# A halved K load, an earlier maximum and a finer last weight load in a decode-attention kernel that streams 1.08 GB

## Chip, cores, metric

One core of a Trainium2 chip. The metric is the time of one execution in device microseconds (us).

Names: PE is TensorE's matmul row, DVE is VectorE, ACT ScalarE, SP SyncE, which issues nearly every load. A timeline line reads: start in us, length in us, engine, line of the kernel, operation, output<-inputs, shapes, how many, and in brackets the idle time before it and what ended it. PEq, DVEq and SPq are the engines' sequencers, the parts that wait for semaphores.

## The reference, cut to what matters

```python
x = A_x                                     # 1 x 448
xn = _layernorm(x)
q = (xn @ wq) in 16 heads of 256            # one query per head
scores = q . k_cache * 256**-0.5            # k_cache: 16 x 65536 x 256, bf16
o = softmax(scores) . v_cache               # v_cache: the same size
g = silu(silu(xn @ w1) @ w2)
return x + (o @ wo) * g
```

K and V are 537 MB each and are read once. Each head is cut into four blocks of 16384 keys, 64 blocks in all, 8 MiB of K and 8 MiB of V per block.

## The kernel before

Three buffers `R[0..2]` of 8 MiB hold everything. A K block is multiplied in place by VectorE and summed by VectorE and ScalarE; then its V block is loaded over it, TensorE multiplies V by the weights, and the next K block but two is loaded over that. So a K load waits for a V product (`vf`), and a V load for VectorE (`kf`).

```python
def load_k(i, s):
    take(sp, vf[s])                          # SyncE waits: V product of this buffer done
    sp.dma_start(out=R[s][:, :], in_=block(Kd, i)).then_inc(kl[s], 16)
    sp.sem_inc(kh[s], 16)                    # kl: first half there, kh: second half there

def load_v(i, s):
    take(sp, kf[s])                          # VectorE is done with this K block
    sp.dma_start(out=R[s][:, :], in_=block(Vd, i)).then_inc(vl[s], 16)

def pe_v(s):
    take(pe, pv)
    take(pe, vl[s], 16)
    pe_keys(psO, s, s, 0, KB, True, True, od)    # 64 matmuls, two keys a partition each
    pe_mark().then_inc(vf[s], 1)

def pe_max(i):
    pe_rows()              # waits for VectorE's maxima of block i, puts them in one row
    pe_query(i + 1)        # the next block's query, which VectorE needs to start it
    pe_bcast()             # waits for the maximum over the row, sends it to ScalarE

# SyncE
load_k(2, 2); load_v(0, 0); load_v(1, 1)
with nc.Fori(NR, LAST - 2, NR, ...) as i:    # NR = 3, LAST = 63
    for s in range(NR):
        load_k(i + s, s)
        load_v(i + s - 1, (s - 1) % NR)
# ... (last K in halves, last V blocks in pieces) ...
pieces = cuts(0, 5, 10, 14, 16)              # wo's heads, one load and semaphore for each piece

# TensorE
pe_max(0)
with loop(pe, 1, LAST - 2, NR) as i: ...     # pe_turn, pe_max(i), pe_v(s) for three blocks
pe_block(NBLK - 3, 0)
pe_turn()
pe_v(1)                                      # V product of block 61
pe_max(NBLK - 2)                             # maximum of block 62, query of block 63
# ... at the very end, after the last V product:
project(10, 12); pe_turn(...); project(12, 14); project(14, 15); project(15, 16)
```

A block has KB = 128 keys in each partition, and HK is half of that. `pe_turn` transposes the last output row, so head 15 can be projected only after it.

## Time and profile before

| what | before |
|---|---|
| time, median of the first 3 runs | 2521.9 us (2521.62 to 2524.93) |
| span of the traced run | 2521.1 us |
| bytes read | 1084.3 MB, 430 GB/s over the span |
| VectorE busy | 89% |
| an 8 MiB block behind another one | 19.36 us |
| last wo landing, last projection ended | 2514.94, 2516.96 us |

The page has 40 equal slices of 63 us. A slice's GB/s says how full the queue was; that of 433 is what the stream reaches with no hole.

A landing below is an issue's time plus its time to landing.

### The profile page before, as it was taken

To read this page: it belongs to the slowest core of one execution; us is meant where nothing else is said; L and a number is where in the kernel's file an instruction comes from. 1 tells how busy PE (TensorE), PEld (TensorE's weight loads), DVE (VectorE), ACT (ScalarE), POOL (GpSimd) and SP (SyncE) were. 2 spreads that over 40 slices of the span, in tenths; PEclk is the share of its full clock that TensorE was granted. 3 is DMA by queue.
4 is the path that set the end of the run, shared out by engine and by line. 5 is a ranking of instruction groups with operands and counts; after the bars stand their busy time and mean duration, and the time that the engine had idled before them with its cause. 6 is when DMAs were issued, how large, how long until landed. Compare 5 with 4: busy or idle time off the path is not lost. (4 is left out here: it accounts for less than half of the span.)

```text
span 2521.1 us, 29267 instructions
## 1 busy us (share of the span) xinstructions
PE 1151.9 (46%) x4738; PEld 438.2 (17%) x4738; DVE 2233.4 (89%) x10277; ACT 1445.9 (57%) x6996; POOL 1.9 (0%) x14
## 2 busy tenths in 40 slices
PE   3243544534535435345354353453543534534457
PEld 1111211111112112111121121121211211111122
DVE  6979889889898898898988988989989889889897
ACT  4656556556565565565655655655556556556564
POOL 0000000000000000000000000000000000000000
PEclk7666767767667677677676676766766767767678
DMA  9999999999999999999999999999999999999998
GB/s 424 402 433 433 433 433 433 434 432 433 435 434 436 435 436 434 434 433 434 435 433 433 433 433 433 433 433 433 433 436 435 436 436 434 434 433 435 433 423 353
DMA packets 22872, 1084.50 MB, mean 430 GB/s; under 512 B 2371, under 2 KB 4549, under 8 KB 4933
## 3 DMA queue, kind: packets, MB, share of 16 engines
q1 hardware_dynamic: 22850, 1084.30, 99.6%
q8 instruction: 5, 0.08, 0.0%
q14 instruction: 15, 0.11, 0.0%
q10 hardware_dynamic: 2, 0.00, 0.0%
HBM read 1084.29 MB, written 0.00 MB: 430 GB/s over the span
## 5 line engine op out<-in xcount | busy, mean ns | idle before, releaser
L276 ACT ACTIVATE R<-R 128x256 bf16<-128x256 bf16 x3328 | 1330.7, 401 | 754.4 <-ACTq L159 754.3
L254 DVE CUSTOM_DVE_ANT_0 R<-R,qcur 128x256 bf16<-128x256 bf16 x4864 | 1700.2, 417 | 0.0
L323 PE MATMUL bank<-R,PV 128*2 128x512 bf16 x4096 | 1032.1, 419 | 20.9 <-PEq L159 7.6
L243 DVE TENSOR_TENSOR R<-R,qcur 128x3328 bf16<-128x3328 bf16 x256 | 482.6, 1885 | 190.0 <-DVEq L159 189.9
L276 ACT ACTIVATION_READ_ACCUMULATOR R<-R 128x1 f32 x3328 | 619.9, 186 | 0.0
L335 PE MATMUL bank<-ident,rmax 128*1 128x128 bf16 x65 | 17.1, 263 | 1078.9 <-PEq L159 1078.9
L323 PEld LDWEIGHTS bank<-R,PV 128*2 128x2 bf16 x4096 | 367.3, 90 | 657.7 <-issue 218.4
L254 DVE DVE_READ_ACCUMULATOR2_ANT S<- 128x1 f32 x4864 | 384.1, 79 | 0.0
L335 PEld LDWEIGHTS bank<-ident,rmax 128*1 128x1 bf16 x65 | 5.2, 79 | 1083.4 <-issue 1083.3
L352 PE MATMUL bank<-eye,O 2*128 2x2 f32 x264 | 40.0, 252 | 231.3 <-PEq L159 231.3
L289 ACT ACTIVATE hist<-bank 128x1 f32 (+1 forms) x65 | 11.1, 171 | 204.4 <-ACTq L159 204.4
L352 PEld LDWEIGHTS bank<-eye,O 2*128 2x128 f32 x264 | 36.2, 207 | 248.6 <-issue 248.6
L219 DVE TENSOR_REDUCE gmax<-bank 1x1 bf16<-1x128 f32 x65 | 18.3, 281 | 38.1 <-DVEq L159 38.1
L236 DVE CAST qcur<-bank 128x256 bf16<-128x256 f32 x64 | 27.2, 425 | 24.6 <-DVEq L159 24.5
L310 ACT COPY hist<-bank 128x2 f32 (+1 forms) x66 | 10.5, 160 | 59.8 <-ACTq L159 59.8
L302 ACT COPY O<-bank 2x512 f32<-2x512 f32 x67 | 37.5, 559 | 12.4 <-ACTq L159 12.4
L291 ACT ACTIVATE PV<-S,hist 128x128 bf16<-128x128 f32 (+1 forms) x65 | 26.0, 399 | 13.4 <-ACTq L159 13.2
L366 PE MATMUL bank<-q,ident 8*128 (+1 forms) x63 | 24.3, 386 | 7.6 <-issue 1.7
L229 DVE COPY S<-S 128x128 f32<-128x128 f32 (+1 forms) x65 | 14.7, 226 | 9.5
L230 DVE TENSOR_REDUCE rmax<-S 128x1 bf16<-128x128 f32 (+1 forms) x65 | 18.2, 279 | 0.0
L341 PE MATMUL bank<-gmax,ones_row 1*128 1x1 bf16 x65 | 10.3, 158 | 4.6 <-PEq L159 0.9
L291 ACT ACTIVATION_READ_ACCUMULATOR PV<-S,hist (+1 forms) x65 | 12.1, 186 | 0.0
(68 smaller groups left out, 90.6 us busy)
## 6 DMA issues: line engine op xcount, KB each, us to landing
R<-in_A_k_cache_dram SPq DMA_DIRECT2D x4, 4096.0 KB, 24.2
R<-in_A_v_cache_dram SPq DMA_DIRECT2D x6, 2048.0 KB, 21.5
R<-in_A_wq_dram SPq DMA_DIRECT2D x1, 3072.0 KB, 12.7
R<-in_A_v_cache_dram SPq DMA_DIRECT2D x3, 1024.0 KB, 15.2
R<-in_A_wo_dram SPq DMA_DIRECT2D x2, 1120.0 KB, 18.4
R<-in_B_w_dram SPq DMA_DIRECT2D x1, 1568.0 KB, 27.1
R<-in_B_w_dram SPq DMA_DIRECT2D x1, 1344.0 KB, 5.8
R<-in_A_v_cache_dram SPq DMA_DIRECT2D x2, 512.0 KB, 16.4
```

Source lines behind the costliest of these rows:

```text
L219: dve.reduce_max(out=gmax[0:1, :], in_=ps_m[0:1, :], axis=AX.X).then_inc(gm, 1)
L230: dve.reduce_max(out=rmax[:, :], in_=S[:, c0:c1], axis=AX.X).then_inc(rm, 1)
L236: dve.tensor_copy(out=qcur[:, :], in_=ps_q).then_inc(sd, 1)
L243: m = dve.tensor_tensor(out=pair, in0=pair, in1=qcur[:, None, :].to_broadcast([P, NA, Dh]), op=ALU.mult,)
L254: ins = dve.tensor_tensor_reduce(out=Kv[:, c, :], in0=Kv[:, c, :], in1=qcur[:, :], scale=1.0, scalar=0.0, op0=ALU.mult, op1=ALU.add, accum ...
L276: ins = act.activation(out=prod, in_=prod, func=ACT.Identity, accum_out=S[:, c : c + 1],)
L291: act.activation(out=PV[s][:, c0:c1], in_=S2[:, c0:c1], func=ACT.Exp, bias=col(0, 1), scale=scale, accum_out=col(1, 2),).then_inc(pv, 1)
L302: act.copy(out=O[:, :], in_=po).then_inc(oc, 1)
L323: ins = pe.matmul(po, lhsT=PV[t][:, c : c + 2], rhs=R[s][:, c * Dh : (c + 2) * Dh], start=(start and c == k0), stop=(stop and c == k1 - 2),)
L335: pe.matmul(ps_m[0:1, :], lhsT=rmax[:, 0:1], rhs=ident[:, :], start=True, stop=True).then_inc(tm, 1)
L352: ins = pe.matmul(ps_t2[:, 2 * a : 2 * a + 2], lhsT=Ov[:, j, a, :], rhs=eye2[:, j, :], start=(j == 0), stop=(j == 1), is_transpose=True,)
L366: pe.matmul(ps_q, lhsT=ident[0:HP, at(j)].to_broadcast([HP, P]), rhs=q8[:, o : o + Dh] if isinstance(o, int) else q8[:, bass.ds(o, Dh)], s ...
```

## The change

Its intent: keep the queue filled at the one place where it ran empty, and shorten what follows the last landing. Diff, cut:

```diff
+    vh = [sem(f"vh{t}") for t in range(NR)]          # half a V product done
-    pieces = cuts(0, 5, 10, 14, 16)
+    pieces = cuts(0, 5, 10, 12, 14, 16)

-    def load_k(i, s):
+    def load_k(i, s, h=None):
+        if h is not None:
+            take(sp, h)
         take(sp, vf[s])

-    def pe_v(s):
+    def pe_v(s, k=KB, between=None):
...
-        pe_keys(psO, s, s, 0, KB, True, True, od)
+        pe_keys(psO, s, s, 0, HK, True, False, vh[s])
+        pe_keys(psO, s, s, HK, k, False, k == KB, od if k == KB else None)
+        if between:
+            between()
+            pe_keys(psO, s, s, k, KB, False, True, od)

-        with nc.Fori(NR, LAST - 2, NR, ...) as i:
+        take(sp, vh[0])
+        load_keys(R[0], block(Kd, NR), 0, HK, kl[0])     # fourth K block, first half
+        take(sp, vf[0])
+        load_keys(R[0], block(Kd, NR), HK, KB, kh[0])
+        load_v(2, 2)
+        for s in range(1, NR):                           # rest of the first pass, unrolled
+            load_k(NR + s, s, vh[s])
+            load_v(NR + s - 1, s - 1)
+        with nc.Fori(2 * NR, LAST - 2, NR, ...) as i:

-        with loop(pe, 1, LAST - 2, NR) as i: ...
-        pe_block(NBLK - 3, 0)
+        loop(pe, 1, NBLK - 3, NR, pe_block, more=1)      # leaves after one block of its last pass
         pe_turn()
-        pe_v(1)
-        pe_max(NBLK - 2)
+        pe_v(1, 96, lambda: pe_max(NBLK - 2))

-        project(h0, h0 + 2)
+        project(h0, h0 + 1)
         t = pe_turn(tok=True)
...
+        project(*pieces[3])
+        pe.wait_ge(wl[4], 16)
+        project(pieces[4][0], H1)
```

## The prediction

> **What bounds the kernel now.** I read the page's slices first, then the DMA queue's issues in order of time, stretches of 5 us in the first 200 us, the chain of waits, and the last 90 us engine by engine. The slices:
>
> ```profile
> DMA  9999999999999999999999999999999999999998
> GB/s 424 402 433 433 433 433 433 434 432 433 435 434 436 435 436 434 434 433 434 435 433 433 433 433 433 433 433 433 433 436 435 436 436 434 434 433 435 433 423 353
> HBM read 1084.29 MB, written 0.00 MB: 430 GB/s over the span
> ```
>
> The queue carries 433 GB/s nearly everywhere; VectorE, the busiest engine, has 89% and waits for K blocks. So the kernel is bound by moving 1084 MB, and only the slices that fall short can give anything: slice 2 (402), a little of slice 1, and the last two. 1084.3 MB at 433 GB/s is 2504 us; 2521.1 leaves 17 us for start, holes and end. A change that moves no bytes can take only a part of these 17 us, 0.7%.
>
> The hole in slice 2, by the queue's issues and in stretches (columns: span, busy time of PE, PEld, DVE, ACT, POOL, PEclk, DMA share, GB/s):
>
> ```profile
> 60.32 35.82 SPq L202 DMA_DIRECT2D R<-in_A_v_cache_dram  x2
> 117.81 0.35 SPq L197 DMA_DIRECT2D R<-in_A_k_cache_dram  x1
> ...
> 110.00:115.00 5.00, 5.00 (x25) 1.96 (x24) 5.00 (x27) 3.15 (x16) 0.00 (x0) 1.00 1.00 433
> 115.00:120.00 5.00, 3.12 (x17) 1.45 (x15) 5.00 (x24) 1.43 (x6) 0.00 (x0) 1.00 0.73 262
> 120.00:125.00 5.00, 0.00 (x0) 0.00 (x0) 5.00 (x20) 4.95 (x26) 0.00 (x0) 0.52 0.98 419
> ```
>
> The V block issued at 95.8 was the last thing in the queue. The fourth K block is issued only at 117.81, when the V product of block 0 (next fence, 100.64 to 117.5) has freed its buffer. By then the queue runs dry.
>
> ```profile
> 100.64 16.86 PE L323 MATMUL bank<-R,PV 128*2 128x512 bf16 x64 [3.59 <-PEq L159]
> 117.34 0.17 PE L376 MATMUL bank<-ident 128*1 128x1 bf16 x1
> ```
>
> The end, first TensorE and then VectorE:
>
> ```profile
> 2445.57 16.88 PE L323 MATMUL bank<-R,PV 128*2 128x512 bf16 x64 [2.96 <-PEq L159]
> 2462.29 0.17 PE L376 MATMUL bank<-ident 128*1 128x1 bf16 x1
> 2462.32 0.22 PE L335 MATMUL bank<-ident,rmax 128*1 128x128 bf16 x1
> ...
> 2506.51 7.07 PE L323 MATMUL bank<-R,PV 128*2 128x512 bf16 x32
> 2513.87 0.92 PE L699 MATMUL bank<-R,OT 128*1 128x448 bf16 x4 [0.29 <-DMA R<-in_A_wo_dram]
> 2514.72 0.64 PE L352 MATMUL bank<-eye,O 2*128 2x2 f32 x4
> 2515.28 1.68 PE L699 MATMUL bank<-R,OT 128*1 128x448 bf16 x8
> ```
>
> ```profile
> 2459.59 0.28 DVE L230 TENSOR_REDUCE rmax<-S 128x1 bf16<-128x128 f32 x1
> 2462.68 0.28 DVE L219 TENSOR_REDUCE gmax<-bank 1x1 bf16<-1x128 f32 x1 [2.81 <-DVEq L159]
> 2463.83 0.43 DVE L236 CAST qcur<-bank 128x256 bf16<-128x256 f32 x1 [0.87 <-DVEq L159]
> 2464.29 1.89 DVE L243 TENSOR_TENSOR R<-R,qcur 128x3328 bf16<-128x3328 bf16 x1
> ```
>
> ```profile
> 2495.95 17.87 DMA R<-in_A_wo_dram
> ```
>
> VectorE has block 62's maximum at 2459.87, but TensorE is in block 61's V product until 2462.3, so the last block starts at 2464.29. From 2506.51 TensorE works without a pause, and the wo piece with four heads lands at 2513.82, within 0.3 us of TensorE's being ready. The chain of waits names the transfer, but two chains end together there: the queue, and VectorE's last block followed by TensorE's last products. Shortening one alone would gain almost nothing.
>
> **What the Trainium skill says.** [...]the late K block took 23.0 us from issue to landing, where block follows block at 19.36 us (landings of 8 MiB blocks in the stretch after it), so 3.7 us are not its bytes, some of them the rest of the V block ahead. "TensorE: Matmul & The Clock Gate", section "What's actually happening", says that the array's clock falls to half after about 3.4 us of idleness; in this trace 1.98 us idle before 2481.74 was followed by a granted clock of 0.55, while 1.81 us before 2501.88 kept 1.00. "Runtime: NRT & Kernel Launch", section "Instruction fetch mechanics", says that a taken branch to a page that is not held stalls the engine. VectorE's 0.87 us idle before 2463.83, as it leaves its loop, may be one; this trace can't prove it.
>
> **The change part by part.**
>
> 1. Halved fourth K block. The half semaphore comes after 32 of the 64 matmuls. The first run at half clock: stretches of 5 us from 100 hold 11 and 21 of these matmuls, so the 32nd ends near 110. The first 4 MiB are then issued at about 110, some 8 us earlier, while the V block runs to 120.1. The second half is issued at 117.8 as before, behind 9.7 us of backlog. The hole closes. Its size in two ways: V1 lands at 120.11 (95.81 + 24.3), K3 at 140.84 (117.81 + 23.0), that is 20.7 us after it and not 19.36: 1.4 us. By bandwidth, 115 to 120 lacks 171 of 433 GB/s: 2.0 us. I take 1.6 us. VectorE also starts that block on its first half, at about 133 rather than 140.97; its 7.6 us of waiting move to the next K block, as the queue sets the pace from then on. All later landings move 1.6 us earlier.
>
> 2. Maximum ahead. Block 62's maximum, now ready at 2459.87 - 1.6 = 2458.3, is taken after 48 of block 61's 64 matmuls. Those began at 2445.57 - 1.6 and the last 16 take 3.5 us, so the 48th ends near 2457.3: TensorE waits 1 us, too short by the trace for a clock drop. VectorE's last block starts 1.97 us (2464.29 - 2462.32) after that row product, at about 2460.4 and not at 2464.3: 3.9 us earlier, 1.6 from the stream and 2.3 from this part. The 16 matmuls left end 2.1 us later relative to the stream; they free the buffer of the last V block, whose loads are issued behind three blocks' halves and pieces and land 27 us later, so that costs nothing. VectorE's end, hence TensorE's end chain, is ready 3.3 to 3.9 us earlier, and TensorE then waits for the last V pieces instead of for VectorE.
>
> 3. wo in three parts. The last V piece landed at 2494.83 + 16.8 = 2511.6; it now lands near 2510.0. Four matmuls of 0.22 follow, then ScalarE's copy (0.57, from 0.13 after), so the transposes start about 1.8 us after the landing, at 2511.9, and not at 2514.72. Meanwhile head 10 needs only its own two-head piece, about 1.1 us behind the V piece. After the transposes (0.6) come ten projections rather than eight, 0.21 each: end near 2514.6. The last two-head piece, landed at 2496.56 + 18.4 = 2514.95 before, lands near 2513.35; four products after it end at 2514.3. The later of the two, 2514.6, stands against 2516.97 before: 2.4 us.
>
> 4. One more block in TensorE's loop replaces 70 unrolled matmul-class instructions by a compare and branch in each of its passes, 20 of them. Between V products TensorE idles (17.41 us before a row product), so this costs nothing. SyncE gets one more wait per K block, already satisfied: nothing.
>
> Sum: 1.6 us of stream plus about 0.8 us of end, 2.4 us, not 1.6 + 2.3 + 1: parts 2 and 3 only let the end follow the queue. 2521.9 - 2.4 = 2519.5 us.
>
> **Rivals.**
> (a) Only the stream gains: the end stays TensorE's, because VectorE's early start is eaten by ScalarE, which must still copy block 61's output (now later) before it sums the last block. For it: ScalarE works in order. Against: it idles 3 us between groups of sums. Then 1.6 us: 2520.3.
> (b) The end gains in full and the hole too (2.0 us plus 1.3): 2518.5. Against: the last wo piece lands when the queue delivers it.
> (c) TensorE's new branches stall on instruction fetch behind a full queue at the loop's exit, now just before block 61's product. It has about 5 us (2438.95 to 2445.4) before V arrives; a longer stall would delay VectorE's last block and take back part 2: 2521 to 2522.
> (d) Holes reopen in the steady stream because K's release waits on two semaphores. Against: a block in the stretch from 193 us takes 25 us from issue to landing, a backlog of some 2 us. A microsecond per pass would be 20 us, 2540; unlikely.
>
> **Range and chances.** The three runs before span 3.3 us, more than the expected gain, so the range is set by noise and by rivals (a) to (c): 2517.3 to 2522.0. 2% is 50 us, three times all that lies outside the stream, so faster by over 2% is as good as excluded (0.003); slower needs rival (d) several times over (0.007); within 2%: 0.99.
>
> **What would show it.** Step 1: 4 MiB issued near 110 us, slice 2 near 420 GB/s or more, VectorE's fourth block starting near 133. Step 2: the last row product before the last 16 matmuls of block 61; VectorE's last block starting near 2460.4. Step 3: transposes near 2511.9, and last projections within 0.5 us of the last landing plus 0.9. Step 4: no idle time of TensorE over 3 us at its branch. I am wrong if slice 2 stays near 402, if the last landing doesn't move by 1 to 2 us, or if the end keeps its 2.0 us between last landing and last projection.

## The result, and the profile after

| | before | changed |
|---|---|---|
| first median | 2521.98 us (4 runs) | 2521.62 us (4 runs) |
| ratio | | 0.9998 (0.998 to 1.0015) |
| all runs, median | 2522.01 us (31 runs) | 2521.47 us (14 runs) |
| span of the traced run | 2521.1 us | 2519.0 us |

A ratio is the mean time of one kernel's runs over that of the other's of the same rounds, so not quite the ratio of the medians quoted. The pooled medians, from four sessions (the changed kernel ran in three of them), put it 0.54 us lower; resampling the runs gives -1.0 to +0.1 us for that difference, so even its sign is not quite secured. The time was within the predicted range, but the gain is a quarter of the 2.4 us that I had worked out. The first trace of the changed kernel, though, shows almost all of the steps I had named. Slices first:

```profile
DMA  9999999999999999999999999999999999999998
GB/s 424 410 440 431 428 433 433 434 435 433 433 433 435 435 434 434 433 433 433 433 433 433 433 433 433 433 433 433 433 433 434 433 433 434 434 436 433 434 428 357
```

Slice 2 went from 402 to 410 only. I had asked for 420. SyncE's issues and the stretches of 5 us (columns as in the prediction):

```profile
61.47 35.81 SPq L205 DMA_DIRECT2D R<-in_A_v_cache_dram  x2
110.81 7.26 SPq L209 DMA_DIRECT2D R<-in_A_k_cache_dram  x2
```

```profile
95.00:100.00 5.00, 0.81 (x3) 0.28 (x3) 4.00 (x15) 0.99 (x5) 0.00 (x0) 0.50 0.72 249
...
115.00:120.00 5.00, 3.23 (x18) 1.47 (x15) 5.00 (x22) 1.31 (x5) 0.00 (x0) 1.00 0.94 406
```

The first half of the fourth K block is issued at 110.8, 7 us earlier, and the stretch from 115, which had 262 GB/s, has 406. That hole is closed. The dip that remains in slice 2 is an older one, from 95, before the second V block; it was 301 GB/s before. The fourth K block landed at 139.40 and not at 140.84, so this trace seems to show a gain of 1.4 us. The end, TensorE, then VectorE:

```profile
2443.68 12.72 PE L326 MATMUL bank<-R,PV 128*2 128x512 bf16 x48 [3.43 <-PEq L159]
2457.66 0.22 PE L338 MATMUL bank<-ident,rmax 128*1 128x128 bf16 x1 [1.26 <-PEq L159]
...
2458.54 3.61 PE L326 MATMUL bank<-R,PV 128*2 128x512 bf16 x16
...
2511.49 0.54 PE L726 MATMUL bank<-R,OT 128*1 128x448 bf16 x2
2512.28 0.61 PE L355 MATMUL bank<-eye,O 2*128 2x2 f32 x4 [0.25 <-PEq L159]
2512.82 2.05 PE L726 MATMUL bank<-R,OT 128*1 128x448 bf16 x10
```

```profile
2457.23 0.28 DVE L233 TENSOR_REDUCE rmax<-S 128x1 bf16<-128x128 f32 x1
2458.02 0.28 DVE L222 TENSOR_REDUCE gmax<-bank 1x1 bf16<-1x128 f32 x1 [0.51 <-DVEq L159]
...
2459.63 1.89 DVE L246 TENSOR_TENSOR R<-R,qcur 128x3328 bf16<-128x3328 bf16 x1
```

The maximum is taken after 48 matmuls. VectorE has its maxima at 2457.51 and starts the last block 2.12 us later; before it was 4.42 us. The last wo piece landed at 2496.46 + 17.23 = 2513.69, and the last projection ended at 2514.87: 1.18 us after it, where it had been 2.02. Both parts work. The puzzle is that a trace with these gains belongs to a kernel whose runs are hardly faster.

### The profile page after: what moved, and what is told of

Its sections match the earlier page's. It is cut to its first block, busy times and chain, and to the rows that moved or that the text cites. A ratio compares the mean times of both kernels' runs of the same rounds, so it can differ in the third digit from the quotient of the medians.

```text
span 2519.0 us, 29363 instructions
## 1 busy us (share of the span) xinstructions
PE 1149.7 (46%) x4738; PEld 437.6 (17%) x4738; DVE 2233.3 (89%) x10277; ACT 1446.1 (57%) x6996; POOL 1.9 (0%) x14
## 6 DMA issues: line engine op xcount, KB each, us to landing
R<-in_A_wo_dram SPq DMA_DIRECT2D x2, 1120.0 KB, 21.8
```

## Experiments

Theory 1, as in the prediction: the hole costs 1.4 to 1.6 us in every run, the end 0.8 us. Its rivals: the gains are smaller than what runs differ by; or they are made up for, or given back, later in the stream.

**1. The changed kernel again; 2. the K halves alone; 3. the maximum ahead and wo's parts without the halves; 4. a hole made ten times larger.** The first is not edited. For the second, only `vh`, the split in `pe_v` and the SyncE part of the diff are kept. For the third, only `pieces`, the projections and `pe_v(1, 96, ...)`. The fourth, on the kernel before:

```diff
-        with nc.Fori(NR, LAST - 2, NR, ...) as i:
+        load_v(2, 2)              # third V block first,
+        load_k(NR, 0)             # then the fourth K block
+        for s in range(1, NR): load_k(NR + s, s); load_v(NR + s - 1, s - 1)
+        with nc.Fori(2 * NR, LAST - 2, NR, ...) as i:
```

> The changed kernel again, to get the size out of the noise. Theory 1 (the hole and the end): the trace gained 1.25 us at the last landing and 2.1 us at the last projection, so the mean of the fast runs is 1.5 to 2.5 us below the kernel before (ratio 0.9990 to 0.9994). Rival (the gain lies within what runs differ by): ratio 0.9997 to 1.0003, and the traces of two runs of the same kernel differ at the last landing by 1 us or more.

> The kernel before with the fourth K block in halves alone. Theory 1: no hole after the second V block, K3 landing near 139.4 and not 140.8, last landing 1.2 to 1.5 us earlier, but the end chain of TensorE also moves only by that, so span and time 1.2 to 1.6 us below the kernel before. Rival (holes are made up for later in the stream, since engines ahead of the slowest are the ones that idle): the last landing moves by less than 0.5 us.

> Maximum ahead and wo in three parts without the K halves and without the loop's block. Theory 1: the last landing stays where the kernel before has it, the last block on VectorE starts 2.3 us earlier against block 62's maximum, and the time from last landing to last projection falls from 2.0 us to about 1.2 us: span 0.8 us below before. Rival (only the stream gains): last landing to last projection stays 1.8 us or more.

> The kernel before with the fourth K block issued after the third V block (issued near 132) and not before it, so the queue is left empty for a long time: the hole made about ten times larger. Theory 1 (a hole there costs its length, nothing later makes up for it): the next V block lands near 153.7 and not 139.5, a hole near 14 us, and the time is 13 to 15 us over the kernel before. Rival (slack later in the stream takes it up, as VectorE waits 3 us per block): less than half of that, under 7 us.

| run | median us (runs) | kernel before, same rounds | ratio (interval) | last landing to last projection |
|---|---|---|---|---|
| changed, again | 2521.35 (5) | 2522.01 (9) | 0.9997 (0.9984 to 1.0011) | 1.16 us |
| halves alone | 2522.45 (5) | the same | 1.0005 (0.9991 to 1.0018) | 2.04 us |
| maximum and wo's parts | 2520.91 (5) | the same | 0.9996 (0.9983 to 1.001) | 1.23 us |
| hole made larger | 2553.65 (4) | the same | 1.0126 (1.0111 to 1.0142) | |

The end behaves as theory 1 has it: it is short exactly where parts 2 and 3 are in. The halves alone gain nothing that can be seen, where 1.2 to 1.6 us had been expected. Without the halves the kernel is no slower than with them. That speaks against the hole's 1.4 us, but the intervals reach over 3 us either way, so these times alone don't decide it. Run 1's rival came: its ratio is 0.9997, and the last wo piece landed at 2513.69 in the first trace of the changed kernel and at 2514.72 in the second, 1.03 us apart.

The enlarged hole missed its expected 13 to 15 us by a factor of two, upwards, so its rival (under 7 us) falls. SyncE's issues and the stretches there:

```profile
60.52 71.53 SPq L202 DMA_DIRECT2D R<-in_A_v_cache_dram  x3
132.16 18.21 SPq L197 DMA_DIRECT2D R<-in_A_k_cache_dram  x2
207.22 0.33 SPq L202 DMA_DIRECT2D R<-in_A_v_cache_dram  x1
...
120.00:125.00 5.00, 0.00 (x0) 0.00 (x0) 5.00 (x22) 3.94 (x21) 0.00 (x0) 0.67 0.00 0
...
195.00:200.00 5.00, 0.00 (x0) 0.00 (x0) 5.00 (x21) 2.22 (x12) 0.00 (x0) 0.50 0.00 0
```

There are two holes, at 0 GB/s. The V block issued at 131.72 landed at 153.69, 13.8 us late (expected: near 14). The K block behind it came late too, VectorE needs 34.2 us from a K block's landing to the release for its V block, and so the V load at 207.22 came after the queue had run dry again: 17.3 us. Together 31.1 us; the medians differ by 31.6. Nothing later makes up for a long hole. I had overlooked the second one.

So a long hole costs its length, and the short one apparently next to nothing. The shares say why. First and last share of the fourth K block, in all traces but those of runs 4 and 11, which delay blocks, and of run 12, slowed by fetches:

| halves not in | first share | last share | | halves in | first share | last share |
|---|---|---|---|---|---|---|
| before | 139.10 | 140.84 | | changed | 137.57 | 139.40 |
| before, again (run 10) | 137.87 | 139.67 | | changed, again | 136.88 | 139.59 |
| maximum and wo's parts | 138.68 | 140.61 | | changed, third (run 9) | 136.45 | 139.34 |
| loop alone (run 6) | 138.47 | 140.10 | | halves alone | 137.55 | 140.16 |
| maximum alone (run 7) | 138.63 | 139.44 | | no longer loop (run 5) | 137.64 | 140.91 |
| wo's parts alone (run 8) | 138.06 | 139.92 | | | | |
| mean | 138.47 | 140.10 | | mean | 137.22 | 139.88 |

The first share gains 1.25 us, the last one 0.22 us, less than runs differ by. The last of the 16 shares of the second V block, at about 120, is 1.8 to 3.4 us behind the first in every one of these traces (in two of them a second share is as late). The others run dry in the hole; the late one is still busy with that V block, or nearly so. Whoever waits for the load waits for the late share. In the enlarged hole the same arithmetic holds: its first share lost 153.04 - (117.23 + 19.36) = 16.45 us and its last 153.69 - (120.52 + 19.36) = 13.81 us; the late one's lag of 3.3 us shrank to 0.6 meanwhile. Theory 2 therefore: the stream's pace is that of the latest engine, a hole costs what it exceeds that engine's lag by, and the first trace of before showed the hole at its most costly.

Put to the six traces without halves, the rule takes the later of two times: the issue plus 21.8 us (what all fresh shares take in run 11, below), or the V block's last share plus 19.36 us. It gives the K block's last share within 0.1 us in three traces, and 0.4 and 0.5 us too early in two. In the first trace of before it is 1.2 us too early: fifteen shares had landed by 139.69 and the sixteenth at 140.84, with no instruction fetch after 108. What delayed that one is open.

**5. All but the longer loop; 6. the longer loop alone; 7. the maximum ahead alone; 8. wo's three parts alone.** Each keeps the named part of the diff above, on the kernel before.

> Parts 1 to 3 of the change on the kernel before, without the longer loop of TensorE. Theory (the loop part only moves an instruction fetch, gains nothing by itself): a 16 KB fetch near 2353 us as before, the transfer under way then lands about 1 us late, one such late landing fewer at the end; time as the changed kernel's, 2521.0 to 2522.0, last landing to last projection 1.2 us. Rival (the loop part carries gain, since it takes a fetch out of the stream): 1 us or more slower than the changed kernel.

> The longer loop of TensorE alone. Theory: no fetch near 2353 but one near 2436 to 2448, end chain as before (2.0 us from last landing to last projection), hole before the fourth K block as before; time within 0.5 us of the kernel before. Rival: 1 us faster or more, by the fetch that is gone.

> The maximum ahead alone. Theory (parts 2 and 3 only work together): VectorE's last block starts 2.0 to 2.5 us earlier against block 62's maximum, TensorE is ready early and then waits about 2 us or more for the wo piece of four heads, and last landing to last projection stays 1.9 to 2.1 us. Rival (the early maximum is what gains): 1.3 us or less.

> wo's last heads in three parts alone. Theory (parts 2 and 3 only work together): TensorE has no wait for wo's pieces at all, being late itself with the last V product, and last landing to last projection stays 1.8 to 2.2 us. Rival (the split is what gains): 1.3 us or less.

| run | median us (runs) | ratio (interval) | last landing to last projection |
|---|---|---|---|
| without the longer loop | 2521.28 (5) | 0.9997 (0.9984 to 1.0011) | 1.22 us |
| longer loop alone | 2522.04 (5) | 1.0001 (0.9987 to 1.0015) | 2.01 us |
| maximum alone | 2521.55 (1) | | 2.00 us |
| wo's parts alone | 2521.2 (1) | | 1.30 us |

The kernel before had 2521.81 (9 runs) in these rounds. The longer loop moves TensorE's instruction fetches of 16 KB: before they lie at 2353, 2429, 2469 and 2508 us, with it at 2438, 2448 and 2490 (the trace's packets of the instruction queues). The landing 1.11 us late at 2367.51 is gone, one at 2444.58 is 1.54 us late where it had been 0.49, and nothing is gained. That was expected. The other two were to show that parts 2 and 3 help only together. The maximum alone gives:

```profile
2512.41 0.92 PE L701 MATMUL bank<-R,OT 128*1 128x448 bf16 x4 [1.10 <-DMA R<-in_A_wo_dram]
2513.26 0.64 PE L352 MATMUL bank<-eye,O 2*128 2x2 f32 x4
2513.83 1.68 PE L701 MATMUL bank<-R,OT 128*1 128x448 bf16 x8
```

TensorE is ready earlier and waits 1.10 us (I had expected about 2) for the four-head piece, and the transposes and eight projections still stand behind it: no gain. But wo's parts alone shortened the end by 0.7 of the 0.8 us:

```profile
2504.68 7.07 PE L323 MATMUL bank<-R,PV 128*2 128x512 bf16 x32
2511.68 0.54 PE L700 MATMUL bank<-R,OT 128*1 128x448 bf16 x2
2512.58 0.61 PE L352 MATMUL bank<-eye,O 2*128 2x2 f32 x4 [0.36 <-PEq L159]
2513.12 2.05 PE L700 MATMUL bank<-R,OT 128*1 128x448 bf16 x10
```

Here the last V product ends 1.2 us after its last piece landed, at 2510.57. In the first trace of before it was 1.9 us. The difference is in the clock. Before, 2481.8 us, and then the second trace of before (run 10) and the halves alone (run 2) at the same place:

```profile
2481.74 0.22 PE L335 MATMUL bank<-ident,rmax 128*1 128x128 bf16 x1 [1.98 <-PEq L159]
2481.79 5.30 PE L323 MATMUL bank<-R,PV 128*2 128x512 bf16 x16
```

```profile
2479.68 0.22 PE L335 MATMUL bank<-ident,rmax 128*1 128x128 bf16 x1 [1.63 <-PEq L159]
2479.74 3.61 PE L323 MATMUL bank<-R,PV 128*2 128x512 bf16 x16
```

```profile
2480.09 0.22 PE L338 MATMUL bank<-ident,rmax 128*1 128x128 bf16 x1 [1.99 <-PEq L159]
2480.14 3.61 PE L326 MATMUL bank<-R,PV 128*2 128x512 bf16 x16
```

After 1.98 us of waiting for VectorE's maxima the granted clock fell to half, and sixteen matmuls took 5.30 us; after 1.63 and after 1.99 us they took 3.61, so the length of the wait alone doesn't decide it. The drop at this place stands in two of the seven traces without the early maximum (before and run 6) and in none of the seven with it. So "two chains end together" was true of a trace with that drop. In the second trace of before, TensorE is ready and waits 1.14 us for the four-head piece. Without the drop the split alone shortens the end. With it the gain would be lost: by run 8's numbers the end would take 1.30 + (1.9 - 1.2) = 2.0 us, an estimate that no run tests. The early maximum would then be a safeguard: with it TensorE waits 0 to 0.8 us for the maxima at that place (2477.34 in the first trace of the changed kernel: no idle time). The split alone has one run, so I count it as the main part and leave the exact shares open.

**9. The changed kernel a third time; 10. the kernel before again; 11. the fourth K block held back; 12. VectorE's loop nine blocks long.** The last two:

```diff
 # 11, on the kernel before
+        take(sp, vf[0])
+        sp.dma_start(out=spare[0:1, :], in_=A_x[0, 0:1, :]).then_inc(late, 16)
+        sp.wait_ge(late, 16)
+        ...                       # then K block 3, and the rest of the pass unrolled
 # 12, on the changed kernel
-        loop(dve, 0, LAST, NR, lambda i, s: dve_block(s))
+        loop(dve, 0, LAST, 3 * NR, lambda i, s: dve_block(s % NR))
```

> The changed kernel a third time. Theory 2 (the last of the 16 engines sets the stream; the half K block closes a hole of the engines ahead of it only): the fourth K block's first share lands near 137.4, against 138.6 without the halves, its last share anywhere in 139.4 to 141.0 as without them; last landing to last projection 1.15 to 1.25 us; time 0.3 to 0.8 us below the kernel before. Rival (the hole's full 1.6 us is gained and the earlier runs were unlucky): 2 us or more below the kernel before.

> The kernel before, for another trace of its hole. Theory 2: the fourth K block's first share lands in 138.0 to 139.1, its last share in 139.4 to 140.9, so that the first trace's 1.4 us of delay for the last share is the upper end of what runs show; last landing to last projection near 2.0 us. Rival (the hole costs the last share 1.4 us in every run): last share 140.6 or later.

> The kernel before with the fourth K block held back until a tiny transfer issued behind the same buffer's release has landed, so it is issued some 2 to 4 us later (near 120.5). Theory 2 (a hole costs only what exceeds the last engine's lag, and beyond that one for one): its last share lands at issue plus 22.0 us, near 142.5, about 2.5 us later than without, and its shares land within 1 us of one another, since all engines start afresh; the time rises by 1.5 to 3.5 us. Rival (slack further on takes it up): under 1 us.

> The changed kernel with VectorE's loop nine blocks long and not three, the same work in the same order; its code no longer stays in the engine's instruction memory, so it is fetched anew in every pass, about 80 fetches of 8 KB more. Theory 2 (fetches take time of one transfer engine, and the stream waits for the last of the 16): 25 to 80 us slower. Rival (fetches are hidden, 0.65 MB of 1084): under 3 us slower.

| run | median us (runs) | ratio (interval) |
|---|---|---|
| changed, third | 2521.47 (5) | 0.9994 (0.998 to 1.0007) |
| before, again | 2521.82 (1) | |
| K held back | 2523.47 (4) | 1.0003 (0.9988 to 1.0019) |
| VectorE's loop of nine blocks | 2608.86 (4) | 1.0339 (1.0323 to 1.0355) |

The runs of the kernel before were scattered in these rounds (2521.86 to 2528.3, median 2522.34), so their ratios say less than usual. Runs 9 and 10 landed their shares near where theory 2 expects them: run 9's first share a microsecond earlier and its last 0.06 us below the range, run 10's first 0.13 us below it. Run 10's last share, at 139.67, rules out its rival (140.6 or later). The last landing to the last projection is 1.17 and 2.01 us.

Run 11 missed its size: the tiny transfer landed after 1.2 us and not after 3, so K was issued at 118.39. But the rule held. Its last share landed 21.8 us after the issue, at 140.22, and its 16 shares within 0.54 us of each other, where the other traces without halves have 0.8 to 1.9: all engines started afresh. The median is 1.5 us above the pooled 2522.01 and 1.1 above its own rounds', so the rise of 1.5 to 3.5 us that was expected isn't shown. Its last share was only 0.1 us later than the mean without halves, so most of that 1.5 us isn't the hole. One microsecond of it can be seen: this kernel, like the changed one, has SyncE's first pass unrolled, and SyncE's loop code is fetched at 219 and 225 us, not at 102 and 108 as before. With all shares together, the effect of these two fetches stands alone. When the trace's packets are chained by start and length into 16 rows (an inference, as they don't name their engine either), both fetches fall into one row, and the packets behind them take 2.78 and 2.83 us where others take 2.42. The V block that was under way landed at 237.94, fifteen shares within 0.5 us, the sixteenth 1.5 us after the first and the load 0.99 us late. In the changed kernel these fetches are at 217 and 223, in the middle of the stream.

In run 12 such fetches are paid in full. The queues of the changed kernel and of run 12 (packets, MB, share of the 16 engines):

```profile
q14 instruction: 14, 0.11, 0.0%
```

```profile
q1 hardware_dynamic: 23010, 1084.30, 98.1%
q14 instruction: 94, 0.77, 0.1%
```

80 packets of 8 KB more, 0.65 MB in 1084, and 87.4 us (2608.86 - 2521.47): 1.09 us for each. Over half of the blocks land 20.2 to 20.6 us after the one before and not 19.36; the last share is mostly 4 to 5.7 us behind the first, at most 6.6. VectorE itself isn't held up: from a K block's landing to the release of its V load takes 34.35 us (340.90 to 375.25), with the three-block loop 34.2; the median over the run is 34.25 in both. In the chained packets VectorE's fetches lie in the row that is last already: at 202.24 a fetch of 0.33 us, then a packet of 3.08 us in place of 2.42. Only that share is late by it, but the stream goes at its pace.

**What was gained and given back.** In the 13 blocks after the fourth K block, up to 400 us, the landings fall behind a pace of 19.36 us by 0.0, 0.9, 0.7, 1.0 and 2.1 us in the five traces with halves of the table, and by 0, 0.3, 1.0, 0, -0.1 and 0 in the six without: 0.75 us more on average. The last wo landing is at 2514.25 on average without halves and at 2514.74 with them (2514.24 without run 5, whose traced execution took 2524.0 us). So the stream gained nothing from the halves, and the end gained 0.8 us. That fits the 0.54 us of the pooled medians. The moved fetches are the smaller part of what is given back: the V blocks under way at 217 and 223 are 0.1, -0.1, 0.6, 0.5 and 0.0 us late, 0.2 on average. The cause of the rest stays open.

No kernel of the study beats the changed one outside of the noise. Without the halves (run 3) it has 2520.91 and with them 2521.35 in the same rounds: I would leave them out, for simplicity and not for time.

## Why the prediction was right or wrong

- **Bound.** Right. The stream carries 433 GB/s throughout, and no part changed that; the time moved by 0.02%.
- **Step 1, the size.** This is the term that failed. "The hole closes" was right (262 to 406 GB/s, first half issued at 110.8, VectorE starting at 134.5 where 133 was predicted). "Its size in two ways: 1.4 us ... 2.0 us. I take 1.6 us" was not: the last share gained 0.22 us on average. My first way was a single trace with the costliest hole of the six; the second averaged over 16 engines, and an average says nothing of the one that is waited for. Part of the first trace's 1.4 us, a share 1.15 us behind the other fifteen, stays without a cause.
- **Step 2.** The early start was right: 2.12 us from maxima to start, with 2.1 predicted (2458.3 to 2460.4). TensorE's wait was 1.26 us with no clock drop, where 1 us was predicted. By itself the part gained nothing (run 7).
- **Step 3.** Size right: 0.8 us predicted, 2.02 to 1.18 measured. "Shortening one alone would gain almost nothing" holds for the maximum and fails for wo's parts, which gave 0.7 us alone. I had taken a clock drop of one trace for the rule; two of seven have it.
- **Step 4.** The loop costs nothing and gains nothing: right. "SyncE gets one more wait per K block: nothing" looked at the wait and overlooked the unrolled pass, whose code fetches moved from before the hole into the stream (0.2 us on average in five traces).
- **Rivals.** (a), only the stream gains, is the reverse of what came: only the end gained. (b) asked for more of both and falls. (c), a fetch stall at TensorE's branch, fell (its V product began 0.13 us after its data), but fetches do matter, by another way: through the transfer engine they use. Nor were VectorE's 0.87 us before 2463.83 a fetch: the trace has none between 2436.4 and 2467.5. (d), holes in the steady stream because K's release waits on two semaphores: the landings do fall behind by 0 to 2 us, but by up to 1 us without the halves too, and nothing shows the second semaphore as the cause.
- **Signs of being wrong.** By the first trace none came true: slice 2 rose to 410, the last landing moved 1.25 us, the end fell to 1.18 us. Over all traces the second did: the last landing didn't move. One trace was too few for a sign of this size.
- **Range and chances.** The median lay inside, and "same" had 0.99. But the unchanged kernel's 2521.98 lies inside too, so this says nothing for the mechanism. The width was right for the wrong reason: not only noise in the runs, but a stream whose slowest share varies by 1.5 us from run to run.

## What to carry to other kernels

A load lands when the last of its 16 shares does, so before closing a short hole in a full queue, look whether the last share would have run dry in it; a mean GB/s can't tell. Take a second trace before you size a microsecond. Count code that is fetched, not only data: with the queue full, a fetch delays one of the 16 shares, even if the engine that fetches has slack. Here 80 more of them cost 1.09 us each, and two that moved cost 1 us together where all shares were level and 0.2 us on average where they weren't.

## What the Trainium skill lacked or had wrong

- "Runtime: NRT & Kernel Launch", section "Instruction fetch mechanics": it speaks of the stall of the engine that fetches and calls crossing a block boundary mostly hidden. It lacks what a fetch does to a saturated data queue: 80 more fetches of 8 KB cost 87.4 us, 1.09 us each, with VectorE itself not held up.
- "DMA: Bandwidth & Descriptors", section "Why a DMA increments its semaphore by 16 and not by 1": it says that the engines finish independently, but not how far apart. Here 0.5 us when all start afresh (run 11), 4.0 to 4.3 us after the first 100 us, up to 6.6 us with many fetches (run 12).
- "TensorE: Matmul & The Clock Gate", section "What's actually happening": it has the clock fall after at least one idle window of about 3.4 us. Here the window need not be idle: in the 3.41 us before the clock fell at 2482.20, TensorE was busy for 1.43 us. Nor does the longest wait decide it: the clock fell after 1.98 us (sixteen matmuls in 5.30 us) and did not after 1.99 us in run 2 (3.61 us).
